# A causal convolution on TensorE as four 64x64 array tiles, with a new list of chunks, batches and copy engines, in a gated linear recurrence kernel

## The chip, the core and the metric

The kernel runs on one core of a Trainium2 chip. The metric is the device time of one execution in microseconds (us); the median of three timed runs before the change is 365.71 us (362.11 to 367.31). A core has TensorE (PE in the profile, with its weight loads as PEld), VectorE (DVE), ScalarE (ACT), GpSimd (POOL) and SyncE (SP), which issues the DMAs here. Each engine takes its instructions in the order in which the program wrote them.

## The reference

Two layers follow each other over a batch of 4 sequences of 6336 steps with 256 channels. The first is a gated linear recurrence, the second a gated linear unit whose gate is a causal convolution of 5 taps per channel.

```python
log_a = 8.0 * sigmoid(r_gate) * log(clip(sigmoid(a_param), 1e-06, 1 - 1e-06))
a_t = exp(log_a)
x_gated = sqrt(maximum(1 - a_t * a_t, 1e-06)) * sigmoid(i_gate) * x
for t in range(S):
    h = a_t[:, t] * h + x_gated[:, t]
    y[:, t] = h
gate = sigmoid(sum(conv_w[k] * shifted(y, K - 1 - k) for k in range(5)))
out = (gate * (y @ w_val)) @ w_out
```

All inputs and the output are float32, and x, r_gate, i_gate and out are 26 MB each.

## The kernel before

The four sequences are laid behind each other as 25344 rows and cut into **tiles** of 512 rows (the last has 256) and **chunks** of two tiles (the first chunk has one tile, the last 256 rows). A chunk goes through these steps, one function each; their names are the job names of the planner, and in the profile the name ahead of the arrow is the tile that an instruction writes.

- `load` (L224, SP): r_gate and i_gate into `ri`, x into `xt`, 512 KB each for a tile. `NIN` is 3, so three tiles can be in flight. `store` (L447) goes through the same SP queue, in program order.
- `tanh` (L302, ACT): both gates of a tile in one instruction, 128x2048 elements, into `tri`.
- `u2` (L309 and L311, POOL): (tanh + 1) * x into `uring`.
- `srT` (L290, PE): 8 transposes of the r half, for a chunk and one half h of the 256 channels, into a PSUM tile with a single buffer. From here channels lie on partitions and time along the free axis.
- `exp` (L324, ACT): a_t into `aring`, one instruction for a chunk and half. `e` (L332, POOL): its square. `sq` (L337, ACT): the square root, for several chunks in a row, because ACT needs another function table for it; each such batch costs two table loads (ACT_TABLE_LOAD).
- `uT` (L348, PE) transposes `uring` into the PSUM tile `xg`, which has a single buffer; `xg` (L357, DVE) multiplies it by the root, and `scan` (L367, DVE) runs the recurrence into `yring`.
- `conv` (L392, PE): the 5 taps of a tile as matmuls with 128x128 diagonal weights, moving 512 columns, accumulated in `gp`, one job for each half h; `gp` has a single buffer of two banks. `tg` (L399, ACT): the gate's tanh.
- `val` (L407, PE): y @ w_val, 4 matmuls. `gv` (L417, DVE): (tg + 1) * val. `out` (L429, PE): gv @ w_out for 256 rows (a piece), 4 matmuls into `ops`, single buffer. `osb`: the copy from PSUM, on DVE (L440) or ACT (L442).

The order of instructions comes from `make_plan`. It holds a table of costs for the jobs, steps a clock, and at each step takes the job that can start first, ties broken by a priority. It writes the jobs in the order of their planned starts, and each engine then executes its own in that order. Three rules in it matter here. A batch of square roots is begun when the back half (`scan` and what follows) has little left to do; `MIN_UNIT` sets the least number of chunks. `OSB_ENGINE` says for the first 80% of the pieces that DVE copies them, for the rest that whichever of DVE and ACT is free first does. The rings `aring`, `ering`, `uring` (10 tiles) and `yring` (8 tiles) bound how far the front half (`load` to `sq`) may run ahead of the back half.

Of the kernel before, what the change touches and what calls it, by code (L numbers as in the profile page):

```python
# [8 lines left out]
P = 128  # L9
WIN = 512  # L10
CHUNK = 1024
FIRST = 512
SUB = WIN // P
CONV_K = 5
C_SCALE = 8.0
NS = 10
# [4 lines left out]
MIN_UNIT = [1, 1, 2, 2]  # L21

COST = dict(load=(0.1, 3.8), tanh=(0.2, 1.7), u2=(0.25, 3.2), srT=(0.05, 0.45), exp=(0.25, 0.86), e=(0.1, 1.8),
            sq=(0.2, 1.71), uT=(0.05, 0.45), xg=(0.17, 1.07), scan=(0.21, 2.14), conv=(0.05, 1.17), tg=(0.19, 0.83),
            val=(0.02, 0.93), gv=(0.15, 1.07), out=(0.02, 0.47), osbD=(0.15, 0.54), osbA=(0.16, 0.43),
            store=(0.1, 1.2))
TABLE, SEM, DMA_LAT = 1.3, 0.15, 2.2
LEAD = 2.6
OSB_ENGINE = "D" * 40 + "B" * 10
# [6 lines left out]
class Shape:  # L36


    def __init__(self, total, seq):
        self.chunks, self.tiles, self.chunk_of, self.frac = [], [], [], []  # L40
        t = 0
        while t < total:
            n = min(FIRST if t == 0 else CHUNK, total - t)
            if n > WIN and n % CHUNK:
                n = WIN
            c = len(self.chunks)
            g0 = len(self.tiles)
            for o in range(0, n, WIN):
                self.tiles.append((t + o, min(WIN, n - o)))
                self.chunk_of.append(c)  # L50
                self.frac.append(min(WIN, n - o) / WIN)
            self.chunks.append((t, n, g0, len(self.tiles)))
            t += n
        self.off = (CHUNK - FIRST) // WIN
        self.seq, self.total = seq, total
# [6 lines left out]
def make_plan(shape):  # L62

    frac, chunk_of, chunks = shape.frac, shape.chunk_of, shape.chunks
    nw, nch = len(frac), len(chunks)
    size = [n / CHUNK for _, n, _, _ in chunks]
    nq = [max(1, round(2 * f)) for f in frac]  # L70
    pieces = [(g, i) for g in range(nw) for i in range(nq[g])]
    qlast = [sum(nq[:g + 1]) - 1 for g in range(nw)]
    done, nxt, free = {}, {}, {}
    order, units = [], []
    mode = "E"

    def at(op):
        return nxt.get(op, 0)

    def ring(g0, slots):  # L80
        return chunk_of[g0 - slots] if g0 >= slots else -1

    while True:
        cands = []

        def cand(op, eng, deps, prio, i, f, n=1, cost=None):
            t = 0.0
            for d in deps:
                if d[1] < 0:
                    continue  # L90
                if d not in done:
                    return
                t = max(t, done[d] + SEM)
            fix, per = COST[cost or op]
            dur = fix + per * f
            if eng == "ACT" and op != "osb" and (op == "sq") != (mode == "S"):
                dur = dur + TABLE
            cands.append((max(free.get(eng, 0.0), t), prio, op, eng, dur, i, n))

        nsq = at("sq")  # L100
        g = at("load")
        if g < nw:
            cand("load", "DMA", [("tanh", g - NIN), ("u2", g - NIN)], 0, g, frac[g])
        g = at("tanh")
        if g < nw:
            old = g - NTRI
            cand("tanh", "ACT", [("load", g), ("srT", 2 * chunk_of[old] + 1 if old >= 0 else -1), ("u2", old)],
                 3, g, frac[g])
# [5 lines left out]
        if k < 2 * nch:  # L114
            cand("srT", "PE", [("tanh", chunks[k // 2][3] - 1), ("exp", k - 1)], 0, k, size[k // 2])
# [369 lines left out]
```

## Time and profile before

The profiled execution took 365.4 us; its span, from the first to the last instruction, is 363.6 us, so 1.8 us lie around it. It stands 0.3 us under the median of the three timed runs.

| Engine | busy us | share of the span | instructions |
|---|---|---|---|
| ACT | 292.5 | 80% | 226 |
| PE | 289.8 | 80% | 1963 |
| DVE | 286.2 | 79% | 260 |
| POOL | 262.8 | 72% | 160 |

DMA moved 104.43 MB, 287 GB/s over the span, and the mean granted TensorE clock is 0.946 of full speed. Every instruction has a row in the trace; a group's row gives its total busy time and the mean of one in ns, and then the time for which the engine stood idle just before such an instruction, with what ended that. A row of a timeline gives the start and the duration in us. A row of a table of windows gives, for a stretch of the span, each engine's busy time with its number of instructions, then the granted clock, the busy share of the DMA engines and GB/s.

### The profile page before, as it was taken

How to read it: one execution, taken by the hardware profiler on the slowest of the kernel's cores; microseconds unless marked ns; L12 is line 12 of the kernel's file. 1: busy time of each engine (PE TensorE's matmuls, PEld its weight loads, DVE VectorE, ACT ScalarE, POOL GpSimd, SP SyncE). 2: the span in 40 equal slices, each digit the busy share in tenths (PEclk: the TensorE clock that was granted, in tenths of full speed). 3: DMA queues.
4: the chain of work that ended last, by engine and by line, in shares of the span. 5: the costliest groups of instructions: out<-in, count | busy, mean ns of one | idle time of the engine just before them, and what ended most of it. 6: DMA issues, size and time to landing. Idle time of an engine off the chain costs nothing.

```text
span 363.6 us, 5325 instructions
## 1 busy us (share of the span) xinstructions
PE 289.8 (80%) x1963; PEld 185.2 (51%) x1963; DVE 286.2 (79%) x260; ACT 292.5 (80%) x226; POOL 262.8 (72%) x160
## 2 busy tenths in 40 slices
PE   0284957958969949799598599798999698899984
PEld 0143536536645726466355366564555465556643
DVE  3336368966979977989879889999788899699972
ACT  5889797897997898997978988999969978245433
POOL 2889978998979978799998799697999694000000
PEclk9998598987989989999989899999999999899999
DMA  7996969999699889899979986999799822123223
GB/s 243 408 408 249 372 227 353 306 296 399 242 366 362 303 327 409 296 376 320 342 305 368 362 319 237 329 395 397 278 372 352 299 96 104 58 101 133 117 115 144
DMA packets 29384, 104.43 MB, mean 287 GB/s; under 512 B 3239, under 2 KB 3758, under 8 KB 29358
## 3 DMA queue, kind: packets, MB, share of 16 engines
q1 hardware_dynamic: 28814, 103.83, 77.1%
q0 software_dynamic: 544, 0.26, 0.5%
q8 instruction: 15, 0.25, 0.3%
q14 instruction: 11, 0.09, 0.1%
HBM read 78.39 MB, written 25.95 MB: 287 GB/s over the span
## 4 chain that ended last, share of the span: by engine, by line
PE 39%; ACT 29%; DVE 11%; issue 10%; DMA 5%; POOL 2%; ACTq 0%; SPq 0%; DVEq 0%; POOLq 0%
PE gp L392 18%; ACT tri L302 8%; PE xg L348 8%; ACT ering L337 6%; DVE yring L367 6%; DMA ri<-in_i_gate_dram 5%; PE ops L429 5%; PE val L407 4%; ACT tg L399 4%; PE srT L290 3%; ACT aring L324 3%; ACT L337 3%; DVE xg L357 2%; ACT L399 2%; DVE gv L417 1%
## 5 line engine op out<-in xcount | busy, mean ns | idle before, releaser
L392 PE MATMUL gp<-yring,diag 128*128 128x512 bf16 (+11 forms) x572 | 133.4, 371 | 18.4 <-ACT tg L399 18.3
L311 POOL TENSOR_TENSOR uring<-t,xt 128x1024 bf16<-128x1024 f32 (+1 forms) x50 | 116.7, 2334 | 4.2
L332 POOL TENSOR_TENSOR ering<-aring 128x1024 f32<-128x1024 f32 (+2 forms) x52 | 93.6, 1812 | 21.1 <-ACT aring L324 18.1
L367 DVE TENSOR_TENSOR_SCAN yring<-aring,yring,xg 128x1024 bf16<-128x1024 f32 (+4 forms) x50 | 108.0, 2160 | 0.5
L302 ACT ACTIVATE tri<-ri 128x2048 bf16<-128x2048 f32 (+1 forms) x50 | 93.5, 1888 | 2.2 <-DMA ri<-in_i_gate_dram 2.2
L392 PEld LDWEIGHTS <-diag 128*128 128x128 bf16 x572 | 55.7, 105 | 67.6 <-issue 29.6
L357 DVE TENSOR_TENSOR xg<-xg,ering 128x1024 f32<-128x1024 f32 (+2 forms) x52 | 61.3, 1178 | 31.3 <-PE xg L348 19.9
L348 PE MATMUL xg<-ident_b,uring 128*128 128x128 bf16 x396 | 57.8, 334 | 29.0 <-DVE yring L367 23.4
L324 ACT ACTIVATE aring<-srT,khf 128x1024 f32<-128x1024 bf16 (+2 forms) x52 | 60.4, 1162 | 20.6 <-PE srT L290 19.8
L417 DVE SCALAR_TENSOR_TENSOR gv<-tg,val 128x1024 bf16<-128x1024 bf16 (+1 forms) x51 | 60.2, 1182 | 15.9 <-ACT tg L399 14.3
L399 ACT ACTIVATE tg<-gp 128x1024 bf16<-128x1024 f32 (+1 forms) x50 | 50.6, 1013 | 22.5 <-PE gp L392 22.2
L440 DVE COPY osb<-ops 128x512 f32<-128x512 f32 x82 | 55.6, 679 | 15.3 <-PE ops L429 15.2
L429 PE MATMUL ops<-wo,gv 128*128 128x256 bf16 x396 | 61.0, 277 | 6.1 <-DVE osb L440 2.3
L348 PEld LDWEIGHTS <-uring 128*128 128x128 bf16 x396 | 45.3, 138 | 40.0 <-issue 21.6
L309 POOL TENSOR_SCALAR t<-tri 128x1024 f32<-128x1024 bf16 (+1 forms) x50 | 51.8, 1036 | 14.9 <-ACT tri L302 13.5
L407 PE MATMUL val<-yring,wv 128*128 128x512 bf16 (+1 forms) x200 | 51.1, 378 | 0.0
L429 PEld LDWEIGHTS <-gv 128*128 128x128 bf16 x396 | 38.5, 102 | 24.6 <-issue 8.0
L337 ACT ACTIVATE ering<-ering,b 128x2048 bf16<-128x2048 f32 (+2 forms) x26 | 49.9, 1920 | 1.2 <-POOL ering L332 0.2
L290 PE MATMUL srT<-ident_b,tri 128*128 128x128 bf16 x396 | 35.0, 234 | 14.1 <-ACT tri L302 9.9
L290 PEld LDWEIGHTS <-tri 128*128 128x128 bf16 x396 | 29.7, 107 | 24.5 <-ACT tri L302 10.7
L407 PEld LDWEIGHTS <-wv 128*128 128x128 bf16 x200 | 19.5, 99 | 15.2 <-issue 0.8
L442 ACT COPY osb<-ops 128x512 f32<-128x512 f32 x17 | 9.9, 584 | 17.3 <-PE ops L429 10.1
(29 smaller groups left out, 55.5 us busy)
## 6 DMA issues: line engine op xcount, KB each, us to landing
ri<-in_r_gate_dram SPq DMA_DIRECT2D x49, 512.0 KB, 6.3
ri<-in_i_gate_dram SPq DMA_DIRECT2D x49, 512.0 KB, 7.1
xt<-in_x_dram SPq DMA_DIRECT2D x49, 512.0 KB, 6.4
out_dram<-osb SPq DMA_DIRECT2D x49, 512.0 KB, 3.8
ri<-in_r_gate_dram SPq DMA_DIRECT2D x1, 256.0 KB, 4.3
ri<-in_i_gate_dram SPq DMA_DIRECT2D x1, 256.0 KB
xt<-in_x_dram SPq DMA_DIRECT2D x1, 256.0 KB
out_dram<-osb SPq DMA_DIRECT2D x1, 256.0 KB
```

The costliest lines, as they stand in the source:

```text
L290: nc.tensor.transpose(out=dst[:, col:col + P], in_=src[:, j, h * P:(h + 1) * P], identity=ident_b[:])
L302: nc.scalar.activation(out=tri[:, :, 0:nj, :], in_=ri[:, :, 0:nj, :], func=ACT.Tanh, scale=0.5)
L311: nc.gpsimd.tensor_tensor(out=uring[:, g % NS, 0:nj, :], in0=t1[:, 0:nj, :], in1=xt[:, 0:nj, :], op=ALU.mult)
L324: nc.scalar.activation(out=aring[:, h, a0:a0 + nt].rearrange("c (w p j) -> c w p j", p=P, j=nj), in_=live.pop(("srT", k))[:, 0:nt].rearran ...
L332: nc.gpsimd.tensor_tensor(out=ering[:, h, a0:a0 + nt], in0=a, in1=a, op=ALU.mult)
L337: nc.scalar.activation(out=nring[:, :, 2 * a0:2 * a0 + nt], in_=ering[:, :, a0:a0 + nt], func=ACT.Sqrt, scale=-0.25, bias=b025[:, 0:1])
L348: nc.tensor.matmul(out=xg[:, o:o + (P - 1) * nj + 1:nj], lhsT=uring[:, g % NS, j, h * P:(h + 1) * P], rhs=ident_b[:], start=True, stop=True)
L367: nc.vector.tensor_tensor_scan(out=yring[:, h, y0 + c0:y0 + c1], data0=aring[:, h, a0 + c0:a0 + c1], data1=xg[:, c0:c1], initial=0.0 if fr ...
L392: nc.tensor.matmul(out=gp[:, h, c0:c1], lhsT=diag[:, h, kk, :], rhs=yring[:, h, src:src + c1 - c0], start=(sh == 0), stop=(kk == 0 and k = ...
L399: nc.scalar.activation(out=tg[:, :, 0:nt], in_=live.pop(("gp", g))[:, :, 0:nt], func=ACT.Tanh, scale=0.5)
L407: nc.tensor.matmul(out=val[:, m, 0:nt], lhsT=wv[:, hk, m * P:(m + 1) * P], rhs=yring[:, hk, y0:y0 + nt], start=(hk == 0), stop=(hk == H - 1))
L429: nc.tensor.matmul(out=ops[:, e, :], lhsT=gv[:, 2 * i + e, hk, :], rhs=wo2[:, hk, :], start=(hk == 0), stop=(hk == H - 1))
```

## The change

The convolution is written as 64x64 pieces of the TensorE array. A diagonal 128x128 weight has only two nonzero 64x64 blocks, m = 0 and m = 1. For each tap four matmuls are issued, for m in 0, 1 and h in 0, 1: rows 64m to 64m+63 of `yring` for half h, against the block m of the diagonal, into partitions 64h to 64h+63 of bank m of `gp`. So the four use four different quarters of the array; the two of one m write the same bank in different partitions. The convolution of a tile becomes one job instead of two.

Channels thereby come out in another order: bank m, partition 64h+c holds channel 128h+64m+c. The columns of w_val and the rows of w_out are permuted to match as they are loaded, so `gv` needs no change; for this their loads on POOL become 4 and 2 DMAs instead of 1 and 1.

The chunks are now a list: 256 rows, 512, 23 chunks of 1024, 512, 256, 256. The places in the rings are worked out from it. The batches of square roots are a list too (`UNITS`, 15 batches; before the planner formed 13), and a string says for every one of the 99 pieces which engine copies it: 58 on DVE and 41 on ACT (82 and 17 before). Priorities and costs in the planner are other numbers; the planner keeps its principle.

```diff
-FIRST = 512
+CHUNKS = [[256], [512]] + [[512, 512]] * 23 + [[512], [256], [256]]
+UNITS = [1, 2, 2, 2, 2, 2, 3, 3, 2, 2, 2, 1, 1, 1, 2]
-MIN_UNIT = [1, 1, 2, 2]
-LEAD = 2.6
-OSB_ENGINE = "D" * 40 + "B" * 10
+OSB = ("ADADADADDDDDDDDDDDDDDDDDDADADDDDDDDDADAAAADDDDDAADAADDDAADADDADADADADDAAAAADAAADADDADDDDAD"
+       "DAAAAAAAA")
+PRIO = dict(load=5.13, store=-0.06, tanh=3.86, exp=-0.46, sq=-2, tg=-0.7, srT=0.17, uT=-2, conv=0.26, val=6,
+            out=-0.57, e=1.19, u2=4.62, xg=4.5, scan=6, gv=1.35, osb=-2)
...
-        nc.gpsimd.dma_start(wv[:], moe_w_val.rearrange("(hk p) n -> p hk n", p=P))
+        for hk in range(H):
+            for m in range(H):
+                nc.gpsimd.dma_start(wv[:, hk, m * P:(m + 1) * P].rearrange("p (h c) -> p h c", h=H),
+                                    moe_w_val[hk * P:(hk + 1) * P, :].rearrange("p (h m c) -> p m h c", h=H, m=2)[:, m])
-        nc.gpsimd.dma_start(wo[:], moe_w_out.rearrange("(hk p) n -> p hk n", p=P))
+        for h in range(H):
+            nc.gpsimd.dma_start(wo[64 * h:64 * h + 64, :, :],
+                                moe_w_out[h * P:(h + 1) * P, :].rearrange("(m c) n -> c m n", m=2))
...
                 for k, (c0, c1, src) in enumerate(parts):
-                    nc.tensor.matmul(out=gp[:, h, c0:c1], lhsT=diag[:, h, kk, :],
-                                     rhs=yring[:, h, src:src + c1 - c0],
-                                     start=(sh == 0), stop=(kk == 0 and k == len(parts) - 1))
+                    for m in range(2):
+                        for h in range(H):
+                            rows = slice(64 * m, 64 * m + 64)
+                            nc.tensor.matmul(out=gp[64 * h:64 * h + 64, m, c0:c1], lhsT=diag[rows, h, kk, rows],
+                                             rhs=yring[rows, h, src:src + c1 - c0], start=(sh == 0),
+                                             stop=(kk == 0 and k == len(parts) - 1))
```

The order of the instructions moves on every engine. Two places matter most.

First ACT, late in the kernel, with some five chunks still to come. `tri` is the front half's tanh, `aring` its exp, `ering` the square root, `tg` the gate, `osb` a copy. Before, the stretch from the last batch of square roots but one reads:

```order
L337 ACT_TABLE_LOAD
L337 ACTIVATE ering<-ering,b_89 128x2x1024 x3
L399 ACT_TABLE_LOAD
L399 ACTIVATE tg<-gp 128x1024
L324 ACTIVATE aring<-srT,khf 128x1024
L302 ACTIVATE tri<-ri 128x2048 x2
L399 ACTIVATE tg<-gp 128x1024
L324 ACTIVATE aring<-srT,khf 128x1024
```

Now, from the batch that begins with the 22nd chunk:

```order
L315 ACT_TABLE_LOAD
L315 ACTIVATE ering<-ering,b_89 128x2x1024 x2
L428 COPY osb<-ops 128x512
L385 ACT_TABLE_LOAD
L385 ACTIVATE tg<-gp 128x1024
L428 COPY osb<-ops 128x512
L302 ACTIVATE aring<-srT,khf 128x1024
L385 ACTIVATE tg<-gp 128x1024
L428 COPY osb<-ops 128x512
L302 ACTIVATE aring<-srT,khf 128x1024
```

Copies, which stood on ACT only behind its last batch of square roots, now stand between the front half's instructions: 33 of the 41 come ahead of the last batch.

Second, ACT's end. Before, from the last exp:

```order
L324 ACTIVATE aring<-srT,khf 128x256 x2
L399 ACTIVATE tg<-gp 128x1024
L337 ACT_TABLE_LOAD
L337 ACTIVATE ering<-ering,b_89 128x2x1024 x2
L337 ACTIVATE ering<-ering,b_89 128x2x256
L399 ACT_TABLE_LOAD
L399 ACTIVATE tg<-gp 128x1024 x3
L442 COPY osb<-ops 128x512
```

Behind this follow 8 more `tg` and 16 more copies. Now:

```order
L302 ACTIVATE aring<-srT,khf 128x256
L428 COPY osb<-ops 128x512
L315 ACT_TABLE_LOAD
L315 ACTIVATE ering<-ering,b_89 128x2x256 x2
L385 ACT_TABLE_LOAD
L385 ACTIVATE tg<-gp 128x1024
L428 COPY osb<-ops 128x512
L385 ACTIVATE tg<-gp 128x1024
L428 COPY osb<-ops 128x512 x2
L385 ACTIVATE tg<-gp 128x2x256
```

Behind this follow 5 more copies and one more `tg`. The last batch holds 512 rows instead of 2304, and 4 gates remain behind it instead of 11.

More of the change, by code (lines that the diff above doesn't have):

```diff
@@ L210 @@
     shape = Shape(B * S, S)
-    tiles, chunks, chunk_of = shape.tiles, shape.chunks, shape.chunk_of
-    plan, pieces = make_plan(shape)
+    tiles, chunks, chunk_of, pieces = shape.tiles, shape.chunks, shape.chunk_of, shape.pieces
+    plan = make_plan(shape)
     const = ctx.enter_context(tc.tile_pool(name="const", bufs=1))
@@ L318, in op_srT, with op_exp @@
             live["srT", k] = srT
[L320 removed]
+        def op_exp(k, eng):
             c, h = k // 2, k % 2
[L322 to L323 removed]
+            nt, a0 = chunks[c][1], shape.apos[c]
+            nj = tiles[chunks[c][2]][1] // P
             nc.scalar.activation(out=aring[:, h, a0:a0 + nt].rearrange("c (w p j) -> c w p j", p=P, j=nj),
```

294 lines of the change are left out of this document (131 added, 163 removed).

## The prediction

> **What bounds the kernel now.** I read the page's busy times first, then a table of windows that cuts the span where the stages change, then the waits of the middle window.
>
> ```profile
> PE 289.8 (80%) x1963; PEld 185.2 (51%) x1963; DVE 286.2 (79%) x260; ACT 292.5 (80%) x226; POOL 262.8 (72%) x160
> ```
>
> ```profile
> 0.00:20.00 20.00, 3.75 (x20) 2.70 (x21) 7.05 (x19) 14.85 (x13) 11.10 (x14) 1.00 0.91 333
> 20.00:300.00 280.00, 231.64 (x1608) 149.20 (x1607) 230.32 (x201) 249.09 (x180) 248.05 (x142) 0.94 0.89 324
> 300.00:363.60 63.60, 54.44 (x339) 33.26 (x336) 48.82 (x41) 28.53 (x34) 3.65 (x5) 0.96 0.27 110
> ```
>
> The columns after the length are busy us of PE, PEld, DVE, ACT, POOL, then granted clock, DMA share, GB/s. Three engines tie at 80% over the span, but the stages differ. From 20 to 300 us ACT (249.1 of 280) and POOL (248.1) lead; in the last 63.6 us POOL is done, ACT is busy for 28.5 us, and PE (54.4) and DVE (48.8) carry what is left. So the kernel is a front half bound by ACT and a long tail in which ACT has little to do. What keeps ACT from 100% in the middle:
>
> ```profile
> ACT aring L324 <- PE srT L290: 19.2, 19, 2.4
> PE gp L392 <- ACT tg L399: 16.6, 9, 4.3
> ACT tg L399 <- PE gp L392: 7.4, 7, 1.9
> ACT tri L302 <- DMA ri<-in_i_gate_dram: 2.2, 3, 0.9
> ```
>
> Of ACT's 30.9 idle us in this window, 26.6 end with PE: exp waits for transposes that stand behind convolutions in PE's queue, and the gate waits for the convolution. The second row is the way back: PE waits for the gate to free `gp`. The tail begins here:
>
> ```profile
> 303.34 4.79 ACT L337 ACTIVATE ering<-ering,b 128x2048 bf16<-128x2048 f32 x3
> 308.15 1.28 ACT L399 ACT_TABLE_LOAD   x1
> 359.77 0.59 ACT L442 COPY osb<-ops 128x512 f32<-128x512 f32 x1 [0.68 <-PE ops L429]
> ```
>
> The last square root ends at 308.1 us, and the span ends 55.5 us later. ACT has spent 271.0 us busy up to there (14.85 + 249.09 + 1.02 of a gate + 1.28 + 4.79) and 37.1 idle (5.2 before 20 us, 30.9 in the middle, 1.0 behind). The prediction is a sum of three parts: ACT's work up to its last square root, its idle time up to there, and the tail.
>
> **The convolution.** PE's rows at normal clock, start and duration:
>
> ```profile
> 286.89 1.24 PE L392 MATMUL gp<-yring,diag 128*128 128x512 bf16 x5 [1.41 <-ACT tg L399]
> 287.96 0.60 PE L429 MATMUL ops<-wo,gv 128*128 128x256 bf16 x4
> 293.13 1.25 PE L392 MATMUL gp<-yring,diag 128*128 128x512 bf16 x9
> 294.21 0.61 PE L290 MATMUL srT<-ident_b,tri 128*128 128x128 bf16 x8
> L392 PEld LDWEIGHTS <-diag 128*128 128x128 bf16 x572 | 55.7, 105 | 67.6 <-issue 29.6
> ```
>
> Five matmuls of 512 columns take 287.96 - 286.89 = 1.07 us, 0.214 each, so a tile's ten take 2.14 (the last row's 1.24 holds 0.17 of drain that the next matmul overlaps). The nine of a window cut at a ring's end take 1.08: four more pairs of load and matmul cost next to nothing (0.01 us), so the number of instructions is not the bound here, and the 105 ns loads lie hidden under running matmuls.
>
> Now a tile has 20 matmuls of 512 columns. The trace has none on part of the array, so I bound them. If the four of a tap stream together, the tile takes 5 x 0.214 = 1.07; if each takes the whole array, 20 x 0.214 = 4.28. They share neither array cells nor PSUM addresses, which speaks for the low end, and I add that the array may have to empty when it changes between whole and quartered use: two drains of 0.17. I take 1.07 + 0.34 = 1.4 us, a saving of 0.74 per 512 rows, or 37 us of PE over 49.5 such tiles. None of this is a term of the sum by itself; it matters through ACT's waits on PE. In the middle window the convolution holds 104.9 of PE's 231.6 busy us:
>
> ```profile
> 20.00:300.00 280.00, 104.86 (x443) 38.79 (x38) 0.94 0.89 324
> ```
>
> At 1.4 instead of 2.14 this is 69, and PE's share falls from 83% to some 70%. The chance that a transpose finds the queue full falls faster than the load: busy over free goes from 4.8 to 2.3. I let the 26.6 us fall to 11 (bounds 0 and 27).
>
> Two rules of the Trainium skill speak against the low end. "TensorEngine Tiling (Array Packing)", Tiling Modes, says that a change of the tiling mode drains TensorE; that is the 0.34 above, and no run here shows it yet. "TensorE: Matmul & The Clock Gate", Part 3, says a weight load overlaps a running matmul only when its row group differs. The rows above disagree for the whole array, where every load and matmul uses all rows and five pairs still take 1.07; were it so for the quarters, it would be the first rival below.
>
> **ACT's work up to the last square root.** Rows by shape:
>
> ```profile
> L302 ACT ACTIVATE tri<-ri 128x2048 bf16<-128x2048 f32 x49 | 92.4, 1905 | 2.2 <-DMA ri<-in_i_gate_dram 2.2
> L302 ACT ACTIVATE tri<-ri 128x1024 bf16<-128x1024 f32 x1 | 1.1, 1068 | 0.0
> L324 ACT ACTIVATE aring<-srT,khf 128x1024 f32<-128x1024 bf16 x48 | 57.7, 1203 | 18.0 <-PE srT L290 18.0
> L324 ACT ACTIVATE aring<-srT,khf 128x512 f32<-128x512 bf16 x2 | 1.6, 778 | 1.4 <-ACT tri L302 0.7 <-PE srT L290 0.7
> L324 ACT ACTIVATE aring<-srT,khf 128x256 f32<-128x256 bf16 x2 | 1.1, 562 | 1.1 <-PE srT L290 1.1
> L337 ACT ACTIVATE ering<-ering,b 128x2048 bf16<-128x2048 f32 x24 | 48.1, 2002 | 1.1 <-POOL ering L332 0.2
> L337 ACT ACTIVATE ering<-ering,b 128x1024 bf16<-128x1024 f32 x1 | 1.1, 1147 | 0.0
> L337 ACT ACTIVATE ering<-ering,b 128x512 bf16<-128x512 f32 x1 | 0.7, 722 | 0.0
> L399 ACT ACTIVATE tg<-gp 128x1024 bf16<-128x1024 f32 x49 | 50.1, 1021 | 22.5 <-PE gp L392 22.2
> L399 ACT ACTIVATE tg<-gp 128x512 bf16<-128x512 f32 x1 | 0.6, 597 | 0.0
> L337 ACT ACT_TABLE_LOAD x13 | 16.7, 1283 | 0.2
> L442 ACT COPY osb<-ops 128x512 f32<-128x512 f32 x17 | 9.9, 584 | 17.3 <-PE ops L429 10.1 <-issue 7.2
> ```
>
> - Smaller chunks at the ends: one tanh of 1.905 becomes two of 1.068 (+0.2); two exp of 1.203 become two of 0.778 and four of 0.562 (+1.4); one root of 2.002 becomes one of 1.147 and two of 0.722 (+0.6). Together +2.2.
> - Batches: 32 table loads up to there instead of 28, 4 x 1.283 = +5.1.
> - Gates: 47 of 51 now come ahead of the last root, before 39 of 50: 7 x 1.021 + 0.597 = +7.7. This is work out of the tail.
> - Copies: 33 of 41 come ahead, before none: 33 x 0.584 = +19.3. DVE loses 24 copies in all.
>
> 271.0 + 34.3 = 305.3 us.
>
> **ACT's idle time up to there.** Start: 5.2 us. The first tile is half as large, so its two gates bring 0.5 MB less, some 1.5 us at the first window's 333 GB/s. Against this stand the weights:
>
> ```profile
> 1.44 0.90 POOL L242 DMA_DIRECT2D wv<-in_moe_w_val_dram  x1
> 2.35 0.72 POOL L244 DMA_DIRECT2D wo<-in_moe_w_out_dram  x1
> 6.60 1.28 ACT L302 ACT_TABLE_LOAD   x1 [2.49 <-DMA ri<-in_i_gate_dram]
> 11.51 2.00 DVE L271 TENSOR_SCALAR wo<-wo 128x512 bf16<-128x512 bf16 x1 [5.05 <-DMA wo<-in_moe_w_out_dram]
> 17.07 0.70 DVE L357 TENSOR_TENSOR xg<-xg,ering 128x512 f32<-128x512 f32 x1 [3.56 <-ACT ering L337]
> ```
>
> Four more DMAs at up to 0.9 us put POOL at some 6.7 us instead of 3.1, which its first wait for a tanh covers (that comes after the table load at 6.6). But the halving of w_out on DVE, which ended at 13.5 with 3.6 us to spare before the first product, starts about 3.6 us later, and everything of DVE is queued behind it; with the smaller first tile the first product could come some 2 to 3 us sooner than before, so it will be late by about that. ACT has cover: between its first root and its first gate now stand a table load, two exps and two tanhs, 1.28 + 2 x 0.778 + 2 x 1.905 = 6.6 us. Without it the 3 us would be ACT's. I take 4.5 for the start in all.
>
> Middle: PE's part 11, the other 4.3 stay. New is that a copy on ACT can be reached before its matmuls are done; then the tanh and exp behind it in ACT's queue wait, and POOL, and at last the loads on SP. Bounds: nothing, or the 17.3 / 17 = 1.0 us of the copy's row, which was measured in a tail where ACT had no other work. Where gates and tanhs stand between, I take 0.15 each, 5 us for 33. With 1.0 as before behind the middle: 4.5 + 11 + 4.3 + 5 + 1.0 = 25.8.
>
> The last square root then ends at 305.3 + 25.8 = 331 us, later than the 308.1 of before.
>
> **The tail.** Behind it DVE has four small products, four small scans, two large and two small gate products (the small ones in two parts each):
>
> ```profile
> L357 DVE TENSOR_TENSOR xg<-xg,ering 128x256 f32<-128x256 f32 x2 | 0.9, 429 | 1.3 <-PE xg L348 1.3
> 348.07 0.75 DVE L367 TENSOR_TENSOR_SCAN yring<-aring,yring,xg 128x256 bf16<-128x256 f32 x1
> L417 DVE SCALAR_TENSOR_TENSOR gv<-tg,val 128x1024 bf16<-128x1024 bf16 x49 | 59.5, 1213 | 15.1 <-ACT tg L399 13.4 <-PE val L407 1.5
> L417 DVE SCALAR_TENSOR_TENSOR gv<-tg,val 128x256 bf16<-128x256 bf16 x2 | 0.8, 418 | 0.9 <-ACT tg L399 0.9
> ```
>
> 4 x (0.43 + 0.75) + 2 x 1.21 + 4 x 0.42 = 8.8. The last tile adds its convolution and gate ahead of its products (0.8 + 0.6), matmuls and copy behind (0.6 + 0.6), the 3.2 us from the last copy's end at 360.4 to the end of the span, and about 1 us of gaps: 15.6. Before, 55.5. If a second large chunk were still open there, one round of two products, two scans, two gate products and its copies would add about 10; that is a bound above.
>
> **The sum.** 305.3 + 25.8 + 15.6 = 346.7 of span, 1.8 around it: 348.5 against 365.4 for the profiled execution, 16.9 less. It lies 0.3 under the median of 365.71, so I predict 348 us. The low end has no waits on PE or for copies (-16) and gives 332. At the high end PE's waits stay at 27 (+16), 364.
>
> **The rivals.**
>
> First, **the weight loads come out** from under the matmuls: a quarter must be empty before it is loaded. With two loads of 105 ns in line a tap takes 0.42, with four 0.63, so a tile 2.1 to 3.2 us, no less than before. Then ACT waits on PE as now (37.1, and 5 for copies), and the time is 305.3 + 42 + 15.6 + 1.8 = 365: no change. For it speaks that the quarters have 20 loads where there were 10; against it, that the present loads are hidden. 10%.
>
> Second, **the copies stall ACT**. It is one mechanism, ACT's queue held by copies whose matmuls are late. With 1.0 us each, as in the row, 33 of them add 28 us to the forecast: 376, slower. It passes 373 from 0.9 us each, and reaches no change from 0.45. For it speaks the row of 17.3 us; against it, that those copies had only gates between them. 8%.
>
> Third, **the quarters run one after the other**, that the change doesn't do what it says. A tile takes 4.28, PE's busy time grows by 49.5 x 2.14 = 106 us to 396, plus 16 at both ends: some 412. PE would be the bound, and slower begins at about 3.5 us a tile. Against it: nothing is shared by the four. 6%.
>
> **How the numbers follow.** The forecast has 76%, and nearly all of it lies under 358.4, the line for faster by over 2% (about what a measurement of this kernel tells from no change); 2 points lie above. Of the first rival 3 points are still faster, 7 the same; of the second 4 the same and 4 slower; the third is slower. Faster 0.77, same 0.13, slower 0.10. The range 332 to 364 holds the forecast and part of the first rival.
>
> **What would show it.** In the new profile the convolution's 20 matmuls should take 1.1 to 1.6 us from their first start to the next group's. ACT should be busy for 313 to 316 us and its last square root should end near 331; exp's wait for transposes should be under 10 us and the copies' wait on ACT under 10; behind the last square root 14 to 18 us should be left. If the convolution takes 2 us or more, or the copies' row shows 15 us of idle time ahead of them outside the tail, the reasoning is wrong at that step.

## The result, and the profile after

The changed kernel takes 349.81 us, the median of four runs (348.21 to 351.18), against 365.12 us for the kernel before in the same measurement: a ratio of 0.9584, 95% interval 0.9501 to 0.9668. In a second measurement, with six runs, it took 349.19 us, 0.952 (0.9467 to 0.9573). The prediction was 348. The profiled execution took 350.42 us, with a span of 348.6. Executions that took over 1.5% longer than the fastest of the same kernel are left out of the medians and ratios here and below. The page's busy times of the kernel after:

```profile
PE 250.4 (72%) x2559; PEld 161.4 (46%) x2559; DVE 270.9 (78%) x247; ACT 310.3 (89%) x262; POOL 266.6 (76%) x170
```

The three engines that tied at 80% have parted: PE has lost 39 us, DVE 15, and ACT, which took over DVE's copies, has gained 18 and stands at 89%. The table of windows of the kernel after (columns as in the prediction; 333.5 lies just behind the last batch of square roots):

```profile
0.00:20.00 20.00, 3.63 (x19) 2.06 (x19) 4.87 (x20) 14.20 (x15) 14.03 (x21) 1.00 0.95 304
20.00:300.00 280.00, 208.08 (x2128) 135.71 (x2128) 225.93 (x186) 259.10 (x205) 236.04 (x136) 0.92 0.88 328
300.00:333.50 33.50, 29.01 (x291) 17.49 (x290) 32.06 (x30) 29.76 (x33) 16.57 (x15) 1.00 0.32 121
333.50:348.60 15.10, 9.72 (x126) 6.09 (x123) 8.01 (x14) 7.21 (x12) 0.00 (x0) 0.97 0.44 175
```

In the middle window ACT is busy for 259.1 us, ten more than before, and has 20.9 us idle instead of 30.9. What ended its idle time there, from the waits of that window:

```profile
ACT aring L302 <- PE srT L268: 7.7, 9, 1.9
ACT tg L385 <- PE gp L377: 6.0, 7, 1.6
ACT osb L428 <- PE ops L415: 4.8, 5, 2.2
ACT tri L280 <- DMA ri<-in_i_gate_dram: 2.5, 1, 2.5
```

The two waits of before, 19.2 for transposes and 7.4 for the convolution, are now 7.7 and 6.0; the copies have brought a third of 4.8. The tail, from the timeline of ACT:

```profile
330.22 1.54 ACT L315 ACTIVATE ering<-ering,b 128x512 bf16<-128x512 f32 x2
331.78 1.28 ACT L385 ACT_TABLE_LOAD   x1
333.07 1.02 ACT L385 ACTIVATE tg<-gp 128x1024 bf16<-128x1024 f32 x1
333.99 0.58 ACT L428 COPY osb<-ops 128x512 f32<-128x512 f32 x1
```

The last square root ends at 331.8 us, 23.6 later than before, and 16.8 us are left behind it, before 55.5. So the kernel does what the sum of the prediction said: more of ACT's work stands ahead of the last root, and most of the tail is gone. And the convolution, PE's rows at normal clock, first a whole tile and what follows it, then one that is cut at a ring's end:

```profile
259.99 1.27 PE L377 MATMUL gp<-yring,diag 64*64 64x512 bf16 x20
261.20 0.61 PE L415 MATMUL ops<-wo,gv 128*128 128x256 bf16 x4
273.53 1.28 PE L377 MATMUL gp<-yring,diag 64*64 64x512 bf16 x36
274.75 1.04 PE L326 MATMUL xg<-ident_b,uring 128*128 128x128 bf16 x8
```

Twenty matmuls take 261.20 - 259.99 = 1.21 us where ten took 2.14; the 36 of this cut tile take 1.22, those of six others of the nine 1.33.

### The profile page after: what moved, and what is told of

It reads as the page before. It is cut to its first block, busy times and chain, and to the rows that moved or that the text cites. A ratio compares the mean times of both kernels' runs of the same rounds, so it can differ in the third digit from the quotient of the medians.

```text
span 348.6 us, 6564 instructions
## 1 busy us (share of the span) xinstructions
PE 250.4 (72%) x2559; PEld 161.4 (46%) x2559; DVE 270.9 (78%) x247; ACT 310.3 (89%) x262; POOL 266.6 (76%) x170
## 4 chain that ended last, share of the span: by engine, by line
PE 31%; ACT 25%; DVE 16%; issue 13%; DMA 11%; POOL 2%; SPq 0%; DVEq 0%; ACTq 0%; POOLq 0%
PE gp L377 12%; PE xg L326 10%; DVE yring L351 8%; ACT tri L280 6%; DMA ri<-in_i_gate_dram 6%; ACT ering L315 5%; DVE xg L335 5%; ACT tg L385 4%; PE ops L415 4%; DMA wo<-in_moe_w_out_dram 4%; ACT L315 3%; PE val L393 3%; ACT L385 3%; PE srT L268 3%; ACT aring L302 2%
## 5 line engine op out<-in xcount | busy, mean ns | idle before, releaser
L351 DVE TENSOR_TENSOR_SCAN yring<-aring,yring,xg 128x1024 bf16<-128x1024 f32 (+5 forms) x54 | 111.1, 2056 | 1.0
L280 ACT ACTIVATE tri<-ri 128x2048 bf16<-128x2048 f32 (+1 forms) x51 | 94.8, 1861 | 3.4 <-DMA ri<-in_i_gate_dram 3.3
L326 PE MATMUL xg<-ident_b,uring 128*128 128x128 bf16 x396 | 58.8, 335 | 41.1 <-DVE yring L351 38.9
L377 PE MATMUL gp<-yring,diag 64*64 64x512 bf16 (+14 forms) x1164 | 72.0, 381 | 22.4 <-ACT tg L385 22.2
L302 ACT ACTIVATE aring<-srT,khf 128x1024 f32<-128x1024 bf16 (+2 forms) x56 | 62.0, 1108 | 9.4 <-PE srT L268 8.9
L415 PE MATMUL ops<-wo,gv 128*128 128x256 bf16 x396 | 62.2, 279 | 10.5 <-DVE osb L426 5.1
L377 PEld LDWEIGHTS <-diag 64*64 64x64 bf16 x1164 | 32.3, 114 | 49.9 <-issue 36.8
L415 PEld LDWEIGHTS <-gv 128*128 128x128 bf16 x396 | 38.6, 105 | 32.1 <-issue 19.2
L426 DVE COPY osb<-ops 128x512 f32<-128x512 f32 x58 | 39.2, 676 | 7.6 <-PE ops L415 7.3
L268 PEld LDWEIGHTS <-tri 128*128 128x128 bf16 x396 | 28.8, 106 | 26.9 <-issue 13.7
L428 ACT COPY osb<-ops 128x512 f32<-128x512 f32 x41 | 24.0, 586 | 9.5 <-PE ops L415 9.2
L393 PEld LDWEIGHTS <-wv 128*128 128x128 bf16 x204 | 19.4, 99 | 16.8 <-issue 4.5
```

What stands on the lines that cost most here:

```text
L268: nc.tensor.transpose(out=dst[:, col:col + P], in_=src[:, j, h * P:(h + 1) * P], identity=ident_b[:])
L280: nc.scalar.activation(out=tri[:, :, 0:nj, :], in_=ri[:, :, 0:nj, :], func=ACT.Tanh, scale=0.5)
L326: nc.tensor.matmul(out=xg[:, o:o + (P - 1) * nj + 1:nj], lhsT=uring[:, g % NS, j, h * P:(h + 1) * P], rhs=ident_b[:], start=True, stop=True)
L351: nc.vector.tensor_tensor_scan(out=yring[:, h, y0 + c0:y0 + c1], data0=aring[:, h, a0 + c0:a0 + c1], data1=xg[:, c0:c1], initial=0.0 if fr ...
L377: nc.tensor.matmul(out=gp[64 * h:64 * h + 64, m, c0:c1], lhsT=diag[rows, h, kk, rows], rhs=yring[rows, h, src:src + c1 - c0], start=(sh == 0),
L393: nc.tensor.matmul(out=val[:, m, 0:nt], lhsT=wv[:, hk, m * P:(m + 1) * P], rhs=yring[:, hk, y0:y0 + nt], start=(hk == 0), stop=(hk == H - 1))
```

## The experiments

The sum landed, but it doesn't show that its causes are right. My theory was that the shorter convolution relieves PE, that ACT's waits on PE fall for that reason, and that the copies fill the time that ACT gains. Then each part should bring something by itself. The rival is that PE, DVE and ACT are tied through their queues, so that relief of one engine moves the wait to another, and only the parts together pay.

### The parts alone

**The whole change with the old convolution.** The order of every engine, the batches and the copies are those of the kernel after; the convolution uses the whole array again, and the two weights are loaded unpermuted.

```diff
-                            nc.tensor.matmul(out=gp[64 * h:64 * h + 64, m, c0:c1], lhsT=diag[rows, h, kk, rows],
-                                             rhs=yring[rows, h, src:src + c1 - c0], start=(sh == 0),
+                        nc.tensor.matmul(out=gp[:, h, c0:c1], lhsT=diag[:, h, kk, :],
+                                         rhs=yring[:, h, src:src + c1 - c0],
```

> The changed kernel with the convolution back on the whole array (10 matmuls of 128x512 for a tile, weights loaded as before) and every other instruction where the change put it. Theory (the convolution pays through the waits on PE): a tile's convolution takes 2.14 us instead of 1.21, PE's busy time rises by about 46 us to 295, ACT's idle time that ends with transposes and convolutions before its last square root goes from 16.5 to 27 us or more, and the time is 360 to 370 us. Rival (the new lists make the gain, the convolution is hidden): under 353 us, with ACT's waits on PE as they are.

Measured: 376.17 us, 1.0254 (1.0196 to 1.0311). From its waits:

```profile
ACT tg L378 <- PE gp L370: 31.5, 25, 4.5
ACT osb L421 <- PE ops L408: 12.7, 17, 2.5
```

With 2.16 us for a tile, ACT's gates wait for the convolution for 31.5 us (8.9 in the kernel after) and its copies for 12.7 (9.2). So without the quarters the new lists and copies lose time, although the unpermuted weights bring the first product at 14.4 us instead of 17.7, if anything a help.

**The quarters alone.** The kernel before, with the quartered convolution and the permuted weights, both halves of a tile issued where the first half's job stood; order, batches and copies are the old ones.

```diff
+            if h == 1:
+                return
+            live["gp", g] = psum.tile([P, H, WIN], FP32, name="gp", tag="gp", bufs=1)
...
-                    nc.tensor.matmul(out=gp[:, h, c0:c1], lhsT=diag[:, h, kk, :],
+                            nc.tensor.matmul(out=gp[64 * h:64 * h + 64, m, c0:c1], lhsT=diag[rows, h, kk, rows],
```

> The kernel before with the convolution as 64x64 quarters (and the weights permuted for it), in the order of before: both halves are issued at the place of the first half's job. Theory: ACT's 28.7 us of waits on PE before the last square root fall by 10 or more, the tail shortens by what PE held up in it, 5 to 10 us of 55, and the time is 345 to 355 us, if DVE with its 82 copies does not take over. Rival (the lists make the gain): 361 to 367 us, because DVE holds the tail.

Measured: 365.98 us, 0.9985 (0.9945 to 1.0026). My theory fell here: the last root ends 4.6 us later than before, and the tail is only 2.7 us shorter. The granted clock does not explain it, since in the executions at 0.942 to 0.947 this kernel took 362.99 to 364.14 us and the one before 363.33 to 366.05. The busy times of this kernel's page:

```profile
PE 257.7 (71%) x2535; PEld 162.4 (44%) x2535; DVE 283.4 (78%) x260; ACT 291.0 (80%) x226; POOL 265.6 (73%) x164
```

And three waits over the whole span, first in the kernel before, then in this one:

```profile
PE xg L348 <- DVE yring L367: 23.4, 17, 4.6
ACT aring L324 <- PE srT L290: 19.8, 20, 2.4
ACT tg L399 <- PE gp L392: 22.2, 17, 5.0
```

```profile
PE xg L353 <- DVE yring L372: 37.5, 25, 6.8
ACT aring L329 <- PE srT L295: 31.2, 20, 4.0
ACT tg L408 <- PE gp L401: 7.5, 4, 2.9
```

PE has 32 us less to do. The gate's wait for the convolution did fall, from 22.2 to 7.5 us, most of it in the tail; but ACT waits longer for PE's transposes, 31.2 us instead of 19.8. In the window of 20 to 300 us the two together rose from 26.6 to 29.6. The other row that rose is PE's own wait for DVE's scan, 37.5 instead of 23.4. How the two hang together can be read at one place of its timeline:

```profile
91.65 2.35 DVE L372 TENSOR_TENSOR_SCAN yring<-aring,yring,xg 128x1024 bf16<-128x1024 f32 x1
94.14 1.03 PE L353 MATMUL xg<-ident_b,uring 128*128 128x128 bf16 x8 [2.56 <-DVE yring L372]
95.10 1.40 PE L401 MATMUL gp<-yring,diag 64*64 64x512 bf16 x36
96.43 0.62 PE L295 MATMUL srT<-ident_b,tri 128*128 128x128 bf16 x8
97.09 1.21 ACT L329 ACTIVATE aring<-srT,khf 128x1024 f32<-128x1024 bf16 x1 [2.44 <-PE srT L295]
```

PE reaches the transposes of u, whose PSUM tile the scan still holds, and stands idle for 2.56 us; the scan ends at 94.00. Behind these in PE's queue come a convolution and then the transposes that exp needs. The profile writes ACT's 2.44 us to PE, and PE is indeed busy during them, but what is late is DVE. I followed every such wait of ACT back along PE's rows to PE's last idle time of over 0.3 us and to what ended that:

| kernel | exp waits for transposes, us | of it with PE held by DVE ahead, us |
|---|---|---|
| before | 19.8 | 6.3 |
| quarters alone | 31.2 | 23.7 |
| after | 8.9 | 4.5 |

The rest, with PE held mostly by ACT itself, did fall with the shorter convolution, from 13.5 to 7.5 us. What took its place is DVE.

**The change with the old copies.** The kernel after in its order, but the first 80 pieces are copied by DVE and the rest as before.

```diff
+COPY = "D" * 80 + "A" * 13 + "D" * 2 + "A" * 4
...
-            if eng == "DVE":
+            if COPY[q] == "D":
```

> The changed kernel with every copy on the engine that had it before (82 on DVE, 17 on ACT at the end), all instructions else in the order of the change; a copy moves to the same place of the other engine's queue. Theory (ACT bounds the front, DVE has slack there): ACT's last square root ends 14 to 19 us earlier than 331.8, DVE's busy time rises by 16 to 287, the tail grows by at least as much since DVE is then behind, and the time is 347 to 358 us. Rival A (DVE has room for all copies): 332 to 340 us. Rival B (the moved copies were the main gain): 360 us or more.

Measured: 374.1 us, 1.0205 (1.0127 to 1.0283). DVE is back at 285.0 us. From its waits:

```profile
ACT tg L387 <- PE gp L379: 34.4, 18, 6.0
PE ops L417 <- DVE osb L428: 22.2, 23, 3.1
ACT aring L304 <- PE srT L270: 17.9, 18, 2.3
```

PE waits 22.2 us (5.1 in the kernel after) for DVE to free the single buffer of the output matmuls, and the gate waits for the convolution behind it. 14 us of work put back on DVE cost some 24 us, and the last root, which my theory had 14 to 19 us earlier, ends at 351.7 us instead of 331.8.

**The same three with an order planned for them.** In the three kernels above, an order stands that was made for other durations. So each was planned anew: the first with the convolution's cost in the planner raised to 1.95, the second with it at 0.56 for a half, the third with the old copies known to the planner. (In the second the rule for the last pieces thereby gives DVE 86 copies.)

```diff
-            sq=(0.3, 1.71), uT=(0.1, 0.65), xg=(0.17, 1.07), scan=(0.21, 2.14), conv=(0.2, 1.1), tg=(0.19, 0.83),
+            sq=(0.3, 1.71), uT=(0.1, 0.65), xg=(0.17, 1.07), scan=(0.21, 2.14), conv=(0.2, 1.95), tg=(0.19, 0.83),
```

> The changed kernel with the convolution on the whole array as in the first experiment, but the planner is told its cost (0.2 + 1.95 us for a tile instead of 0.2 + 1.1), so the order fits it. Theory (the parts need each other: without the shorter convolution PE is as full as DVE and ACT, whatever the order): 358 to 368 us, no gain to speak of. Rival (the first experiment was slow only since its order was made for another kernel): 345 to 355 us, and then the convolution is worth little.

```diff
-            sq=(0.2, 1.71), uT=(0.05, 0.45), xg=(0.17, 1.07), scan=(0.21, 2.14), conv=(0.05, 1.17), tg=(0.19, 0.83),
+            sq=(0.2, 1.71), uT=(0.05, 0.45), xg=(0.17, 1.07), scan=(0.21, 2.14), conv=(0.05, 0.56), tg=(0.19, 0.83),
```

> The kernel before with the quartered convolution, and its planner told the cost (0.05 + 0.56 us for each half's job), old chunks, batches and copy rule. Theory (PE's relief alone becomes waits of PE on DVE, which keeps 80% or more of the copies): 358 to 367 us, tail behind the last square root 45 us or more. Rival (the order was the obstacle): 345 to 355 us.

```diff
-OSB = ("ADADADADDDDDDDDDDDDDDDDDDDADADDDDDDDDADAAAADDDDDAADAADDDAADADDADADADADDAAAADAAADADDADDDDAD"
-       "DAAAAAAAA")
+OSB = "D" * 80 + "A" * 13 + "D" * 2 + "A" * 4
```

> The changed kernel with the old list of copy engines (80 on DVE, then mostly ACT), planned anew for it. Theory (DVE's 16 us of copies, on top of its chain of product and scan, hold the back half): 356 to 368 us, the last square root before 325 us and the tail longer than 25 us. Rival (any order made for its own copies does): 346 to 354 us.

| whole-array or quartered | copies | lists and order | us | ratio (interval) |
|---|---|---|---|---|
| quartered | old | old | 365.98 | 0.9985 (0.9945 to 1.0026) |
| quartered | old, 86 on DVE | old lists, planned anew | 377.93 | 1.0378 (1.025 to 1.0507) |
| whole | new | of after | 376.17 | 1.0254 (1.0196 to 1.0311) |
| whole | new | new lists, planned anew | 368.71 | 1.0135 (1.0015 to 1.0254) |
| quartered | old | of after | 374.10 | 1.0205 (1.0127 to 1.0283) |
| quartered | old | new lists, planned anew | 363.76 | 0.9994 (0.995 to 1.0038) |
| quartered | new | of after | 349.81 | 0.9584 (0.9501 to 0.9668) |

Planning anew helps where the lists are new (by 7 and 10 us); where they are old the kernel lost 12, with four more copies on DVE, and lies above the 358 to 367 us that I had expected. Nowhere does it give a gain over before. In the last row but one, quarters and new lists with the old copies, the last root ends at 312.9 us, 4.8 later than before, and 47 us of tail follow in a span of 360.0:

```profile
311.36 1.54 ACT L314 ACTIVATE ering<-ering,b 128x512 bf16<-128x512 f32 x2
```

The table answers a part of the question. The quarters alone, the copies and lists without the quarters, and the quarters and lists without the copies all bring nothing, in an order made for them or not; with all three the kernel is 4 to 5% faster. So with these lists both the quarters and the copies are needed. The copies alone, the lists alone, and the quarters with the new copies on the old lists were not run, so what the lists themselves are worth stays open.

The clock differs between these kernels too. With the whole array it was granted at 0.942 to 0.953, with the new lists and the old copies at 0.909 to 0.927, with the old lists planned anew at 0.897 to 0.918, and in the kernel after at 0.926 to 0.945. So the loss of the whole-array kernels is not the clock's; of the others it isn't shown how much goes by way of it, nor what cost the second row most.

### Do the quarters run at once?

In the kernel after, the four matmuls of a tap follow each other. Here the loops are turned: five taps of one quarter, then five of the next.

```diff
-            for kk in range(CONV_K - 1, -1, -1):
+            for m, h in ((0, 0), (0, 1), (1, 0), (1, 1)):
+                for kk in range(CONV_K - 1, -1, -1):
```

> The changed kernel with the loops of the convolution turned: all five taps of one quarter, then the next quarter, so that neighbours in PE's queue use the same quarter. Theory (four matmuls stream together because they use different quarters): a tile takes 4.2 to 4.4 us instead of 1.21, PE becomes the bound, and the time is 400 us or more. Rival (a matmul on a quarter is simply shorter): 1.2 us and 350 us.

Measured, in a single execution: 387.19 us. PE's rows of a tile:

```profile
199.79 2.00 PE L376 MATMUL gp<-yring,diag 64*64 64x512 bf16 x20
201.73 1.04 PE L392 MATMUL val<-yring,wv 128*128 128x512 bf16 x4
```

A tile takes 1.94 us: neither the 1.21 of the kernel after nor the 4.28 of twenty in a row, so theory and rival both missed. A cut tile takes 3.22 to 3.54 us in eight of the nine cases and sets this kernel back further. The starts of the single matmuls in the two kernels, worked out from the trace's records, in ns from the first:

```
after:             0    3    7   10 | 242  243  247  250 | 458 ... | 674 ... | 891 ... 899
quarters in line:  0  240  246  457  486  492  673  703  732  738  889  918  948  978 ... 1627
```

In the kernel after, four start within 10 ns and the taps are 216 ns apart (the first 242). In line, a matmul of each further quarter starts about 246 ns after the last quarter's first (0, 246, 492, 738), long before the five of the earlier quarter are through. Were they started in the order of the program, the second and the third, both of the first quarter, would stand 6 ns apart. The records don't name the quarter; that the starts come in four rows of five, 246 ns apart, is read from their spacing. By this reading PE runs ahead from one quarter into the next, and the four work side by side. Within such a convolution PE then doesn't take its matmuls in the order in which the program wrote them, though the text ahead of the prediction says so of every engine. The Trainium skill's "TensorE: Matmul & The Clock Gate", Part 3, has matmuls start strictly in the program's order; by this reading the row disagrees for different quarters. "TensorEngine Tiling (Array Packing)", Tiling Modes, has the tiles of the array operate independently, and there the trace agrees.

### The late weights

In the kernel after, DVE halves w_out ahead of its first product, and the weight comes late. Here the halving is moved behind the second scan of the first chunk.

```diff
-        nc.vector.tensor_scalar(out=wo2[:], in0=wo[:], scalar1=0.5, scalar2=None, op0=ALU.mult)
...
+            if op == "scan" and i == 1:
+                nc.vector.tensor_scalar(out=wo2[:], in0=wo[:], scalar1=0.5, scalar2=None, op0=ALU.mult)
```

> The changed kernel with DVE's halving of w_out moved behind the first chunk's second scan, so that the first product no longer waits for the weights' DMA (it began at 17.7 us; its root was ready at 14.3). Theory (ACT has cover for a late start of the back half): 348 to 350 us, no change against 349.8. Rival (the start sets the end): 3 us less, 346 to 347 us.

Measured: 346.08 us (344.1 to 349.01), 0.9521 (0.9413 to 0.9629). The start of the kernel after, on POOL, DVE, PE and ACT:

```profile
1.44 3.06 POOL L220 DMA_DIRECT2D wv<-in_moe_w_val_dram  x4
4.50 1.21 POOL L224 DMA_DIRECT2D wo<-in_moe_w_out_dram  x2
17.49 0.29 DVE L252 TENSOR_SCALAR wo<-wo 128x512 bf16<-128x512 bf16 x1 [10.89 <-DMA wo<-in_moe_w_out_dram]
17.70 0.43 DVE L335 TENSOR_TENSOR xg<-xg,ering 128x256 f32<-128x256 f32 x1
18.90 0.61 PE L326 MATMUL xg<-ident_b,uring 128*128 128x128 bf16 x2 [6.04 <-DVE yring L351]
19.22 0.71 PE L268 MATMUL srT<-ident_b,tri 128*128 128x128 bf16 x4
19.98 0.78 ACT L302 ACTIVATE aring<-srT,khf 128x512 f32<-128x512 bf16 x1 [1.85 <-PE srT L268]
```

And of the kernel with the late halving:

```profile
14.15 0.43 DVE L334 TENSOR_TENSOR xg<-xg,ering 128x256 f32<-128x256 f32 x1 [7.53 <-ACT ering L314]
324.92 1.53 ACT L314 ACTIVATE ering<-ering,b 128x512 bf16<-128x512 f32 x2
```

The first product comes 3.55 us earlier and the last root ends at 326.45 instead of 331.76 (328.74 in the second profile of the kernel after). ACT's cover, on which the prediction counted, isn't a full one: the wait passes to ACT by the same way as above, since PE stands 6.04 us at the second transposes of u, and those that exp needs are queued behind. In the first 40 us exp's wait for transposes is 3.5 and 3.7 us in the two profiles of the kernel after and 0.5 here, and ACT is busy for 32.2, 31.3 and 34.9 us. That shows the wait at the start. Whether it reaches the end is not resolved: the last roots of the two profiles of one kernel lie 3 us apart, and the ratio, 0.9521, is that of the kernel after in its second measurement, 0.952. The median is the lowest of the study.

The same was done to the kernel with the quarters alone, whose first product also came late (19.25 us, before 17.07).

```diff
-        nc.vector.tensor_scalar(out=wo2[:], in0=wo[:], scalar1=0.5, scalar2=None, op0=ALU.mult)
```

> The quartered convolution in the order of before, as in the second experiment (366 us), with the halving of w_out moved behind the second scan. There the permuted weights' loads held DVE's first product until 19.3 us (17.1 in the kernel before), and the second gate came 5.7 us later than before. Theory (the weights' late arrival ate part of the convolution's gain): first product near 17 us, time 358 to 362 us, 4 to 8 less than in the second experiment; the rest of the convolution's gain is still lost since DVE holds the tail. Rival (the start has nothing to do with it): 364 to 367 us.

Measured: 364.57 us, 0.9951 (0.9912 to 0.9991), 1.4 us under the quarters alone, with the first product at 16.9 us. ACT's wait for transposes is still 29.6 us, 22.0 of it behind DVE. So the late weight was not what had hidden the gain there.

### DVE's work, and ACT's

For the comparison the kernel after was measured once more, unchanged, beside the next two.

> The changed kernel as it is, to stand beside the others of this group: 348 to 351 us.

Measured: 349.19 us, 0.952 (0.9467 to 0.9573).

**More work for DVE.** If DVE sets the pace through PE's queue, work on it must cost time although it is idle for 22% of the span. Twenty multiplications of a scratch tile, whose result nobody uses, are put behind the gate products of tiles 10 to 29.

```diff
+            if 10 <= g < 30:
+                nc.vector.tensor_tensor(out=junk[:, 1, 0:400], in0=junk[:, 0, 0:400], in1=junk[:, 0, 0:400], op=ALU.mult)
```

> The changed kernel with 20 useless multiplications of 128x400 elements on DVE, one behind the gate product of each of the tiles 10 to 29, some 0.5 us each and 10 us together. Theory (front on ACT and back on DVE are balanced, so work on DVE costs time though DVE is idle for 22% of the span): 5 to 12 us more than the changed kernel. Rival (ACT alone bounds it, DVE has slack): 0 to 2 us more.

Measured: 364.72 us, 0.9956 (0.9919 to 0.9993), 15.5 us over the kernel after. The added group (busy time and mean ns behind the first bar):

```profile
L411 DVE TENSOR_TENSOR junk<-junk 128x400 f32<-128x400 f32 x20 | 23.3, 1164 | 0.0
```

And the window of 180 to 240 us, first of this kernel and then of the kernel after in its second profile:

```profile
180.00:240.00 60.00, 44.52 (x434) 28.52 (x439) 53.35 (x44) 44.96 (x39) 45.35 (x26) 0.86 0.77 280
```

```profile
180.00:240.00 60.00, 45.41 (x468) 30.65 (x473) 51.01 (x41) 54.11 (x46) 49.68 (x29) 0.91 0.90 331
```

The twenty took 23.3 us, over twice what I had planned, and cost 15.5: 0.7 us for each us of DVE's work. In the window ACT falls from 54.1 to 45.0 busy us with unchanged work of its own. Two of its waits over the whole span:

```profile
ACT tg L387 <- PE gp L379: 17.2, 11, 5.1
ACT aring L304 <- PE srT L270: 15.0, 13, 3.4
```

In the second profile of the kernel after these were 7.8 and 9.6 us, and the copies' wait rose from 8.2 to 11.0; together the three rose by 17.6 us, about what the kernel lost. Of exp's wait the part behind DVE rose from 5.5 to 11.4 by the method above, which is all of that rise. The granted clock was 0.917 to 0.923, in the kernel after 0.930 to 0.945; how much of the loss goes by way of a slower PE isn't shown.

**Less work for ACT.** The other reading of 89% is that ACT's work now bounds the kernel. Fewer and larger batches of square roots save four table loads, planned anew (on the kernel with the late halving).

```diff
-UNITS = [1, 2, 2, 2, 2, 2, 3, 3, 2, 2, 2, 1, 1, 1, 2]
+UNITS = [1, 2, 2, 3, 3, 3, 3, 3, 2, 2, 1, 1, 2]
```

> The changed kernel with the late halving of w_out and 13 batches of square roots instead of 15, planned anew; 4 table loads less on ACT, 5.1 us. Theory (ACT's work up to its last square root is the bound): 4 to 6 us less than the 346 of the late halving alone, 340 to 343 us. Rival (larger batches keep DVE waiting for roots and lengthen the tail, which gives it back): 345 us or more.

Measured: 366.47 us, 1.0001 (0.9965 to 1.0038), 20 us over the kernel from which it differs by this line and the order planned from it. ACT has 307.1 us of work, 3.3 less, and waits in other places:

```profile
ACT tg L384 <- PE gp L376: 17.9, 16, 2.6
ACT osb L427 <- PE ops L414: 13.6, 15, 2.7
DVE xg L334 <- PE xg L325: 32.1, 22, 3.3
```

These rows were 7.6, 8.3 and 25.1 with the finer batches. The last root ends at 330.6 us instead of 326.5, and 32.4 us are left behind it instead of 16.9: most of the loss is the longer tail that the rival named, while DVE's wait for roots, its reason, stayed at 21 us. So taking work off ACT gave nothing in this order. It doesn't settle whether ACT's work is a bound in another: the order as a whole was planned anew, and the granted clock fell to 0.893, so how much of the 20 us belongs to the batches' size stays open.

## Why the prediction was right, and where its reasons were not

**What bounds the kernel.** "A front half bound by ACT and a long tail in which ACT has little to do" describes where the time was, and the sum built on it held. What it left out is why ACT waits. I read "ACT aring <- PE srT" as PE's load; it is PE's place in line. In the kernel before, 12.2 of the 19.8 us lie behind a PE that waited for ACT itself, the way back that the prediction names, and 6.3 behind DVE; in the quarters alone 23.7 of 31.2 are DVE's lateness passed on by PE.

**The convolution.** Predicted 1.4 us a tile, measured 1.21. 1.07 for the streams was right; the addition of 0.34 for two drains was too large. The records show five taps of 0.216 and about 0.13 for going in and out together. That the 20 loads would not come out was right as well: the records have them under the matmuls, and cut tiles with 36 pairs take 0.01 to 0.12 us longer.

**ACT's work up to the last root.** Predicted 305.3. Up to 333.5 us ACT is busy for 303.06; less the table load and the piece of a gate behind the root (1.28 + 0.43) that is 301.35, 4 us less. The counts were right, 33 copies and 47 gates ahead of the last root. But I added full durations to a busy time that counts overlaps once: neighbouring rows overlap, as 333.07 + 1.02 and the copy at 333.99 show with 0.1 us, and 52 more instructions make up the 4. For the same reason ACT's busy time of 310.3 lies under the 313 to 316 that the prediction named as a sign.

**ACT's idle time up to there.** Predicted 25.8, measured 30.4:

| stretch | predicted | measured |
|---|---|---|
| to 20 us | 4.5 | 5.8 |
| 20 to 300 us, PE's part | 11 | 13.7 |
| 20 to 300 us, copies | 5 | 4.8 |
| 20 to 300 us, the rest | 4.3 | 2.4 |
| 300 us to the last root | 1.0 | 3.7 |

The last root ends at 331.8 instead of 331: 4 us too much work and 4.6 too little idle time offset each other, which is luck. The term for PE has about the right size, but its reason, a shorter queue at PE, doesn't give it. "PE's share falls from 83% to some 70%" happened in the quarters alone, where PE is busy for 205.1 us of the same window, 73%, and ACT's waits on PE there didn't fall (26.6 before, 29.6); they are 13.7 with the new lists and DVE relieved too. The estimate of 0.15 us for a copy was right.

**ACT has cover for the late weights.** This step failed. The halving started 6.0 us later than before (17.49 instead of 11.51), where I had allowed 3.6, and ACT felt it through PE's queue: some 3 us of exp's wait in the first 40 us, gone with the late halving. What it is worth at the end isn't resolved.

**The tail and the sum.** Predicted 15.6, measured 16.8. The sum of 348.5 was made for the profiled execution; with the 0.3 us up to the median it is 348.8, so "I predict 348" rounds it the wrong way.

**The rivals.** The weight loads didn't come out, and copies stalled ACT by 0.18 us each (5.8 for the 33 up to the last root), not 0.45. The quarters do run at once; even in an unfavourable order they take 1.94 us and not 4.28. But the first and the third rival were priced too low. The kernel with the whole array and the new lists takes 2.16 us for a tile, about the first rival's lower figure, and came to 376.17 us, planned anew 368.71, not 365: in the order of after ACT stood idle for 52.9 us up to its last root, where I had 42. And the time did not stay under 373 us up to "about 3.5 us a tile": in that order it was past it at 2.16, and at 1.94, with cut tiles of up to 3.54, it was 387.19 us. A tile of 4.28 was not run. The rival that I should have named is that DVE, at 79%, holds PE's queue: its price is the 366 us of the quarters alone.

## What to carry to other kernels

When several engines tie, follow a wait back through the engine that it names: an engine with a queue in order passes on the lateness of whoever held it, and the profile names only the last one. Relief of one tied engine may then bring nothing (0.9985) while the same relief together with another's, and lists made for both, brings 4 to 5%. So cost such edits together, and test an engine's slack by adding work to it: each us of work added to DVE, which was idle for 22% of the span, cost 0.7 us of time. And where an order is written out in advance, compare edits in an order planned for them as well: here that moved the times by 7 to 12 us, in both directions.

## What the runs showed of the hardware that I had not expected

**DVE waits for POOL when it reads SBUF alone.** The same halving of w_out took 2.00 us in the kernel before, 0.29 in the kernel after and 1.15 with the late halving. The twenty multiplications show why: alone they take 0.56 us, and the 17 that start while a POOL instruction is under way end 0.42 to 0.44 us after it. Rows of the kernel with more work for DVE:

```profile
164.94 2.36 POOL L291 TENSOR_TENSOR uring<-t,xt 128x1024 bf16<-128x1024 f32 x1
165.02 2.71 DVE L411 TENSOR_TENSOR junk<-junk 128x400 f32<-128x400 f32 x1
177.47 1.89 POOL L312 TENSOR_TENSOR ering<-aring 128x1024 f32<-128x1024 f32 x1
178.07 1.72 DVE L411 TENSOR_TENSOR junk<-junk 128x400 f32<-128x400 f32 x1
210.43 0.56 DVE L411 TENSOR_TENSOR junk<-junk 128x400 f32<-128x400 f32 x1
```

POOL's two instructions end at 167.30 and 179.36, DVE's at 167.73 and 179.79. So the 0.56 us of such an instruction became 1.164 on the mean. DVE's other large instructions here have an operand in PSUM, mostly run beside POOL too and keep their time: in the kernel after the 48 gate products of 1024 elements, 43 of them beside a POOL instruction, take 1.19 to 1.22 us, and the 58 copies, 47 of them so, 0.66 to 0.69. The Trainium skill's "SBUF — State Buffer", SBUF: two separate sides, says that DVE with two SBUF inputs, or in a mode with two ports, and GpSimd hold a shared pair of ports for a whole instruction each; the trace agrees.

**Quarters of the array overtake each other.** As read above from the spacing of the starts: matmuls of a later quarter start 246 ns after the earlier quarter's first, ahead of three of its remaining four.
